# Six value pairs beside the second half's logits, and the last chunk's inverse step in three slots

## The chip, the cores and the metric

One core of one Trainium2 chip runs the whole program. The metric is device time in microseconds, the median of the runs shown. Engines are named as in the profile: PE (TensorE matmul), PEld (its weight load), DVE (VectorE), ACT (ScalarE), POOL (GpSimd) and SP (SyncE, which here only issues DMAs).

## The reference

Two independent computations share the program, and their outputs are put side by side.

```python
# A: sliding dilated attention, S = 2048, D = 640, 32 heads of 20, window 8, dilation 2
qkv = x @ wqkv                                   # split into q, k, v
logits[s, w] = q[s] . k[s - 2 w] * 20 ** -0.5    # w = 0..7, masked where s - 2 w < 0
attn = softmax(logits over w)
a = (sum over w of attn[s, w] * v[s - 2 w]) @ wo
# B: long convolution by FFT, L = 2048, D = 640, N = 192
K = Re(sum over n of Cc * exp(dt A l) * dt Bc)   # one filter of length 2048 a channel
y = irfft(rfft(pad(u)) * rfft(pad(K)))[:L] + u * Dskip
out = concatenate([a, y])
```

## The kernel before

Part B works in five chunks of 128 channels. For each chunk it makes the filter (DVE and PE), transforms it, multiplies it with the transformed input (`products`, L348, which loads the input's spectrum from `Sdram` and multiplies it on DVE into P1 and P2), and takes a first inverse step (`inverse_a`, L364). That step has four pieces. Each is 16 matmuls into a PSUM tile `ps_ia`, which ACT then copies to the tile Z (L375). After the fourth piece one DMA on SP's queue writes Z to `Zdram` (L377). The second inverse step (`Inverse.part`, L639, matmuls into `ps_ib`) needs, for one of four quarters of the output positions, the pieces of all five chunks, read back from `Zdram` and `UDdram` by 15 DMAs of 128 KB (`Inverse.load`, L629, issued at L637). Quarter 0's loads are spread over SP and POOL, those of quarters 1 and 2 all go to SP, and quarter 3 is spread again. There are 24 such parts, six to a quarter.

Part A stands beside and after the last chunk. The sequence is handled in two halves of 256 positions on each of four groups. `att.products` (L520, DVE) and `att.logits` (L523, 20 matmuls at L531) make the logits of one window offset w; every second w ACT moves them to SBUF (L534). `softmax_a` (L539) and `softmax_b` (L549) are DVE trees with one ACT exponential between them. Values are made per channel of a head, 20 in all: `proj_v` (L488) makes two channels at once in a two-bank PSUM tile (40 matmuls at L495, one ACT copy at L497), `proj_v1` (L499) one channel in a one-bank tile (20 matmuls, one copy at L506). `v_halo` (L508) copies the positions that a window reaches over a group's edge. `av_step` (L574) multiplies values with attention weights on DVE (L584) and sums over w on PE with identity matmuls (`ps_o`); `p2` runs in a ring of six buffers. `out_piece` (L596) is the output projection (`ps_op`).

The order around the change is partly a scheduler's and partly the program's. Before `att.in_order()` a scheduler places instructions on each engine by its own estimate, with the program's order as its guide. After that call every matmul of the attention object stays in program order (those matmuls all carry the line L420). DMAs are placed by the scheduler throughout, but each engine's queue issues its own in the order that it was given, and a DMA that waits holds up those behind it. SP's queue uses eight completion lanes in turn: a DMA waits until the one eight places before it has landed.

Before the change, the loop over w of the second half's logits (L770 to L783) does `transform(LAST)` at w = 0, `softmax_b(0)` at w = 2, `products` and all four pieces of `inverse_a` at w = 4, and a value pair at w = 1, 3, 5 and 7. Then come the halo of channels 0 to 7, the loads of quarters 0 to 2, and a second loop over w (L799), here called loop 2: `av_step` for the first half's channels 0 to 7, with two single channels each at w = 0 to 5 and four `ps_ib` parts and two halos at w = 4 and 5. After it five blocks of `av_step` follow (L815). The first of them, here called block 1, takes eight `ps_ib` parts, one a step; blocks 2 and 3 take pieces of the output projection instead.

Of the kernel before, what the change touches and what calls it, by code (L numbers as in the profile page):

```python
# [347 lines left out]
def products(tc, pools, Sk, Sd, pool, late):  # L348

    nc = tc.nc  # L350
    P1 = pool.tile([128, 32, 32, 4], bf16, name="P1", tag="sp", bufs=3)
    P2 = pool.tile([128, 32, 32, 4], bf16, name="P2", tag="sp", bufs=3)
    fl = lambda t: t.rearrange("p a b c -> p (a b c)")
    nc.sync.dma_start(out=fl(P1[:]), in_=Sd)
    nc.sync.dma_start(out=fl(P2[0:64]), in_=Sd[64:128])
    nc.sync.dma_start(out=fl(P2[64:128]), in_=Sd[0:64])
    for P in (P1, P2):
        ins = nc.vector.tensor_tensor(out=P[:], in0=P[:], in1=Sk[:], op=A.mult)  # L358
        if late:
            tc.keep_in_program_order(ins)  # L360
    return P1, P2, ins


def inverse_a(tc, pools, C, P1, P2, Zd, pool):  # L364

    nc = tc.nc
    MM = nc.tensor.matmul
    Z = pool.tile([128, 128, 32], bf16, name="Z", tag="sp", bufs=3)

    def piece(b):  # L370
        ps = pools["psum"].tile([128, 8, 128], f32, name="ps_ia", tag="bank2")
        for j in range(8):
            for w, P in enumerate((P1, P2)):
                MM(ps[:, j], lhsT=P[:, 8 * b + j].rearrange("p k g -> p (k g)"), rhs=C["EA"][:, w, :], start=(j % 4 == 0 and w == 0), stop=(w == 1), skip_group_check=True)  # L374
        nc.scalar.copy(out=Z[:, :, 8 * b:8 * b + 8], in_=ps[:].rearrange("p j x -> p x j"))  # L375
        if b == 3:
            nc.sync.dma_start(out=Zd, in_=Z[:].rearrange("p x j -> p (x j)"))  # L377

    return [lambda b=b: piece(b) for b in range(4)]
# [279 lines left out]
def body(tc, ctx, pools, prm, B_u, B_Dskip, Sd, Zd, UDd, A_x, A_wqkv, A_wo, out_a, out_b):  # L659
# [5 lines left out]
    fp = fft.enter_context(tc.tile_pool(name="fft", bufs=1, side="right"))  # L665
# [6 lines left out]
    C = dict(BD=BD, T2=T2, EA=EA, Dsb=Dsb, U=U)  # L672
    R, trig = {}, {}
    with tc.tile_pool(name="prep_b", bufs=1) as pb, tc.tile_pool(name="prep_c", bufs=1) as pc, tc.tile_pool(name="prep_a", bufs=1) as pa, tc.tile_pool(name="psum_p", bufs=2, space=bass.MemoryType.PSUM) as psp:
        pools.update(prep_a=pa, prep_b=pb, prep_c=pc)
        B, fill = partB_prep(tc, dict(pools, psum=psp), prm)
# [17 lines left out]
    att = Attention(tc, pools, A_x, A_wqkv, A_wo, out_a, psk, psg)  # L694
    Kb, Sk = {}, {}

    def transform(c):
        Sk[c] = fwd(tc, pools, C, (lambda ut: Kb[c][:, ut, :]), 1, fp)[0]
# [8 lines left out]
    LAST = NCH - 1  # L707
    for c in range(NCH):
# [6 lines left out]
        if c > 0:  # L715
            P1, P2, last = products(tc, pools, Sk[c - 1], Sd[c - 1], fp, True)
            ia = inverse_a(tc, pools, C, P1, P2, Zd[c - 1], fp)
# [52 lines left out]
    for w in range(W):  # L770
        if w >= 2:
            att.products(1, w)
        att.logits(1, w)
        if w == 0:
            transform(LAST)
        elif w == 2:
            att.softmax_b(0)
        elif w == 4:
            P1, P2, _ = products(tc, pools, Sk[LAST], Sd[LAST], fp, False)
            for f in inverse_a(tc, pools, C, P1, P2, Zd[LAST], fp):  # L780
                f()
        if w in (1, 3, 5, 7):
            att.proj_v(w - 1)  # L783
    att.v_halo(0, 8)
    fft.close()
    att.in_order()
# [4 lines left out]
    parts = inv.parts()  # L791
    rest = []

    def fill(some, n=1):
        for f in some[0:n]:
            f()
        del some[0:n]

    for w in range(W):  # L799
        if w < 6:  # L800
            att.proj_v1(8 + 2 * w)
            att.proj_v1(9 + 2 * w)
            if w in (4, 5):
                fill(parts)
                att.v_halo(*((8, 8) if w == 4 else (16, 4)))
                fill(parts)
        if w == 0:
            att.open_out(a2)
        att.av_step(0, 256, 0, 2, w)
        if w == 2:  # L810
            att.softmax_a(1)
        elif w == 4:
            att.softmax_b(1)
# [20 lines left out]
def kernel(  # L834
# [28 lines left out]
    Zd = dpool.tile([NCH, 128, 4096], bf16, name="Zdram")  # L863
    UDd = dpool.tile([NCH, 128, 2048], bf16, name="UDdram")
    body(tc, ctx, pools, prm, B_u, B_Dskip, Sd, Zd, UDd, A_x, A_wqkv, A_wo, out_a, out_b)


# [28 lines left out]
```

## Time and profile before

| | |
|---|---|
| median of 3 runs | 447.49 us (445.54 to 448.25) |
| the profiled execution's own time | 445.28 us |
| its span | 443.5 us |
| mean granted TensorE clock | 0.915 |
| busy: DVE, PE, ACT, POOL | 392.6, 358.7, 314.6, 41.1 us |
| DMA moved | 51.62 MB, mean 116 GB/s |

Busy time is summed over the whole span, and the stages differ much. The change touches what lies between about 336 and 392 us of the span. A row of the timeline gives start, length, engine, line, operation, output and input tile, count, and in brackets how long the engine was idle before and what ended that. A row SPq is the issue of a DMA on SP's queue, not its transfer.

### The profile page before, as it was taken

The numbers are of one execution on the slowest core, as the hardware profiler recorded it, in microseconds if no ns is written. First come the engines' busy times: TensorE is split into PE (matmuls) and PEld (weight loads), VectorE is DVE, ScalarE is ACT, GpSimd is POOL, SyncE is SP. The second block draws the span as 40 slices with busy tenths as digits, with TensorE's granted clock in tenths as the row PEclk, the third lists the DMA queues.
The fourth block names the chain that finished last, engine by engine and source line by source line (L and its number), as shares of the span: only waits on it lengthen the run. The fifth ranks groups of instructions, "written<-read, shape, count | busy, mean of one in ns | idle before, by whom it ended". The sixth has DMA issues, their size and how long they took to land.

```text
span 443.5 us, 17699 instructions
## 1 busy us (share of the span) xinstructions
PE 358.7 (81%) x8041; PEld 241.5 (54%) x8041; DVE 392.6 (89%) x394; ACT 314.6 (71%) x576; POOL 41.1 (9%) x85
## 2 busy tenths in 40 slices
PE   1385759989878987879687989899997679769896
PEld 0243656867755676457555665544556646424443
DVE  8889999999979999999999889669799989768751
ACT  3984999889998999799997815244486354635653
POOL 7440000000000000000010000000000030503110
PEclk9967888999896999699896989999999699959999
DMA  5589003171251404431299905200004097797243
GB/s 145 185 158 187 5 1 121 38 254 50 96 187 55 98 28 191 143 75 28 120 278 176 248 15 199 98 1 1 1 0 98 2 248 198 196 209 215 82 104 117
DMA packets 45131, 51.62 MB, mean 116 GB/s; under 512 B 31376, under 2 KB 38992, under 8 KB 42368
## 3 DMA queue, kind: packets, MB, share of 16 engines
q1 hardware_dynamic: 41520, 41.41, 35.5%
q0 software_dynamic: 3392, 8.95, 7.2%
q8 instruction: 63, 1.03, 1.0%
q10 hardware_dynamic: 144, 0.12, 0.1%
q14 instruction: 12, 0.10, 0.1%
HBM read 28.03 MB, written 18.35 MB: 105 GB/s over the span
## 4 chain that ended last, share of the span: by engine, by line
PE 44%; ACT 29%; DVE 11%; issue 6%; DMA 5%; SPq 4%; ACTq 0%; POOL 0%; DVEq 0%; POOLq 0%
ACT R L222 10%; ACT A L338 6%; PE ps_k L318 6%; PE ps_ph L247 6%; PE ps_k L323 6%; PE ps_op L420 6%; PE ps_k L464 5%; ACT Sg L344 4%; DVE prod L521 4%; PE ps_ph L250 4%; SPq L637 3%; PE ps_ia L374 3%; DMA Z<-Zdram 3%; PE ps_o L420 3%; PE ps_f L343 2%
## 5 line engine op out<-in xcount | busy, mean ns | idle before, releaser
L305 DVE TENSOR_TENSOR Y<-F,G 128x3072 bf16<-128x3072 bf16 x60 | 103.2, 1759 | 0.4 <-PE ps_k L323 0.3
L222 ACT ACTIVATE R<-LPC 128x192 bf16<-128x192 f32 x225 | 59.3, 359 | 0.1
L247 PE MATMUL ps_ph<-LPC 128*128 128x256 bf16 (+1 forms) x200 | 41.0, 308 | 20.5 <-DMA LPC<-lo 8.0
L318 PE MATMUL ps_k<-Y,X 128*32 128x64 bf16 x1920 | 47.0, 239 | 8.3 <-issue 4.5
L323 PE MATMUL ps_k<-Y,X 64*32 64x64 bf16 x1920 | 43.2, 234 | 2.9 <-issue 2.9
L318 PEld LDWEIGHTS <-X 128*32 128x32 bf16 x1920 | 32.1, 117 | 18.1 <-issue 9.7
L344 ACT CAST Sg<-ps_f 128x1024 bf16<-128x1024 f32 x40 | 37.6, 1025 | 5.8 <-PE ps_f L343 5.8
L338 ACT CAST A<-ps_f 128x1024 bf16<-128x1024 f32 x40 | 37.6, 1032 | 1.6 <-PE ps_f L337 1.4
L584 DVE TENSOR_TENSOR prod<-v,atp 128x2048 bf16<-128x2048 bf16 (+2 forms) x32 | 31.3, 1021 | 8.3 <-PE ps_o L420 5.6
L255 ACT ACTIVATE TX<-ps_ph 128x864 bf16<-128x864 int16 (+1 forms) x40 | 32.3, 864 | 8.2 <-DVE X L271 3.9
L271 DVE TENSOR_TENSOR X<-R,TX 128x1536 bf16<-128x1536 bf16 x40 | 36.5, 958 | 0.0
L343 PE MATMUL ps_f<-A,T 128*128 128x128 bf16 x320 | 23.9, 236 | 14.9 <-ACT A L338 13.5
L323 PEld LDWEIGHTS <-X 64*32 64x32 bf16 x1920 | 29.5, 113 | 11.4 <-issue 4.2
L255 ACT ACTIVATE TA<-ps_ph 128x768 bf16<-128x768 int16 x40 | 30.4, 822 | 2.7 <-PE ps_ph L250 2.4
L247 PEld LDWEIGHTS <-LPC 128*128 128x128 bf16 x200 | 15.1, 102 | 29.0 <-issue 14.1
L343 PEld LDWEIGHTS <-T 128*128 128x128 bf16 x320 | 21.9, 106 | 16.5 <-issue 15.5
L521 DVE TENSOR_TENSOR prod<-ql,kT 128x1024 bf16<-128x1024 bf16 (+1 forms) x24 | 23.1, 1039 | 8.3 <-ACT ql L483 8.3
L250 PE MATMUL ps_ph<-LPC 128*64 128x128 bf16 (+1 forms) x400 | 29.6, 248 | 0.0
L420 PE MATMUL ps_op<-wo,o 128*128 128x320 bf16 x160 | 28.1, 312 | 0.8 <-ACT o L594 0.4
L610 ACT CAST ob<-ps_op 128x320 bf16<-128x320 f32 x28 | 11.9, 431 | 22.1 <-PE ps_op L420 20.4
L375 ACT CAST Z<-ps_ia 128x1024 bf16<-128x1024 f32 x20 | 19.3, 1014 | 11.5 <-PE ps_ia L374 11.5
L374 PE MATMUL ps_ia<-EA,P 128*128 128x128 bf16 x320 | 24.1, 238 | 3.2 <-DVE P L358 3.2
(133 smaller groups left out, 658.8 us busy)
## 6 DMA issues: line engine op xcount, KB each, us to landing
Sdram<-Sg SPq DMA_DIRECT2D x5, 1024.0 KB
P<-Sdram SPq DMA_DIRECT2D x5, 1024.0 KB
P<-Sdram SPq DMA_DIRECT2D x10, 512.0 KB
Zdram<-Z SPq DMA_DIRECT2D x5, 1024.0 KB
Z<-Zdram SPq DMA_DIRECT2D x30, 128.0 KB
U<-in_B_u_dram SPq DMA_DIRECT2D x4, 640.0 KB
UDdram<-UD SPq DMA_DIRECT2D x10, 256.0 KB
out_dram<-ysb SPq DMA_DIRECT2D x32, 80.0 KB
```

The lines of the kernel that those rows point to most:

```text
L222: nc.scalar.activation(out=R[:, :, e, :], in_=src, func=ACT.Exp, scale=m)
L247: MM(o[:, :, 0:32], lhsT=L[:, 0:128], rhs=rhs, start=first, stop=last, skip_group_check=True)
L250: MM(o[64 * hh:64 * hh + 64, :, 32:48], lhsT=L[:, 128:192], rhs=rhs[:, :, 16 * hh:16 * hh + 16], start=False, stop=last, skip_group_check= ...
L255: last = nc.scalar.activation(out=dst[:, qs, e0:e0 + 2 * n, :].rearrange("p q (b e) f -> p b e q f", b=2), in_=words.rearrange("p b (e q f ...
L305: nc.vector.tensor_tensor(out=Y[:].rearrange("p q (b a) f -> p q b a f", a=8), in0=fa, in1=gb, op=A.mult)
L318: MM(ps[32 * g:32 * g + 32, t], lhsT=X[:, q, 2 - k, :, f], rhs=Ys[k][:, q, :, f], start=(t == 0 and k == 0), stop=False, tile_position=(0, ...
L323: MM(ps[32 * g:32 * g + 32, t], lhsT=X[hb, q, 2 - k, :, f], rhs=Ys[k][hb, q, :, f], start=False, stop=(k == 2), tile_position=(64 * (g // ...
L338: nc.scalar.copy(out=A1[:, :, 32 * b:32 * b + 32].rearrange("p k (j g) -> p k j g", g=4), in_=ps[:].rearrange("p j k g -> p k j g"))
L343: last = MM(ps[:, kk], lhsT=C["T2"][:, 8 * b + kk, :], rhs=A1[:, 8 * b + kk, :], start=(kk % 4 == 0), stop=True, skip_group_check=True)
L344: nc.scalar.copy(out=Sg[:, :, 8 * b:8 * b + 8, :], in_=ps[:].rearrange("p k (j g) -> p j k g", g=4))
L420: self.MM = lambda *a, **k: self.tc.keep_in_program_order(self.nc.tensor.matmul(*a, **k))
L521: self.nc.vector.tensor_tensor(out=self.prod[w % (4 - 2 * hf)][:, c0:c1], in0=self.q[hf][:, c0:c1], in1=self.kT[:, hf, c0:c1, :, HALO - DI ...
```

## The change

The order of the value pairs changes. Channels 0 to 11 are now made in pairs within the logits loop: pairs 0, 2, 4, 6, 8 and 10 at w = 1, 2, 3, 4, 5 and 7. The four pieces of the last chunk's `inverse_a`, which all stood at w = 4, are now spread: the first at w = 5 after its value pair, the second at w = 6, the last two at w = 7 after pair 10. The write of Z goes with the last piece. Loop 2 makes the eight channels that are left, at w = 0 to 3, with the halos at w = 3 and 4, and takes five `ps_ib` parts instead of four (one at w = 4, two at w = 5, one each at 6 and 7). No instruction is added or taken away except that two pairs are made by `proj_v` in place of four single channels by `proj_v1`; the matmul count is the same.

```diff
         elif w == 4:
             P1, P2, _ = products(tc, pools, Sk[LAST], Sd[LAST], fp, False)
-            for f in inverse_a(tc, pools, C, P1, P2, Zd[LAST], fp):
+            ia = inverse_a(tc, pools, C, P1, P2, Zd[LAST], fp)
+        if w > 0 and w != 6:
+            att.proj_v((0, 0, 2, 4, 6, 8, 0, 10)[w])
+        if w >= 5:
+            for f in ia[w - 5:w - 4] if w < 7 else ia[2:]:
                 f()
-        if w in (1, 3, 5, 7):
-            att.proj_v(w - 1)
     att.v_halo(0, 8)
...
     for w in range(W):
-        if w < 6:
-            att.proj_v1(8 + 2 * w)
-            att.proj_v1(9 + 2 * w)
-            if w in (4, 5):
+        if w < 4:
+            att.proj_v1(12 + 2 * w)
+            att.proj_v1(13 + 2 * w)
+        if w in (3, 4, 5):
+            if w > 3:
                 fill(parts)
-                att.v_halo(*((8, 8) if w == 4 else (16, 4)))
+            if w < 5:
+                att.v_halo(*((8, 8) if w == 3 else (16, 4)))
+            else:
                 fill(parts)
+        if w > 5:
+            fill(parts)
```

In the built program the change moves these on each engine. PE: the second pair now stands ahead of the logits of w = 3, pairs 4 and 6 ahead of and behind those of w = 4, pair 8 on both sides of those of w = 5; then the first `ps_ia` piece, logits 6, the second piece, logits 7, pair 10, the last two pieces, the halo. DVE: the first `av_step` product goes ahead of the second half's `softmax_a`. ACT: the copies follow PE's order; the first of them for block 2's output pieces now stands ahead of the copy of part 13. SP: five loads of quarter 1 now stand ahead of the write of Z, and quarter 0's loads behind it. POOL: unchanged but for one load of quarter 3, which goes ahead of the first output.

## The prediction

> **What bounds the kernel now.** I read the timelines of PE, SP and POOL from 335 us to the end first, then DVE and ACT, then the stage table (busy time, granted clock and DMA share) and the DMA view.
>
> The hole that the change fills is on PE:
>
> ```profile
> 339.35 2.33 PE L495 MATMUL ps_v<-xT,wv 128*32 128x512 bf16 x39
> 343.87 0.73 PE L531 MATMUL ps_l<-prod,Gs 128*32 128x256 bf16 x20 [2.19 <-DVE prod L521]
> 346.07 0.50 PE L374 MATMUL ps_ia<-EA,P 128*128 128x128 bf16 x3 [1.47 <-DVE P L358]
> 348.28 5.45 PE L374 MATMUL ps_ia<-EA,P 128*128 128x128 bf16 x61 [1.70 <-DVE P L358]
> ```
>
> PE waits 5.4 us in three places for DVE, which is busy without a break from 330 to 354. Later, from 361.5 to 380.7, it is the other way round: PE makes six pairs of single channels, and DVE waits 2.70 us (to 381.31) for the last of them.
>
> What runs beside that are the last chunk's loads:
>
> ```profile
> 354.82 0.33 SPq L377 DMA_DIRECT2D Zdram<-Z  x1
> 357.34 1.92 SPq L637 DMA_DIRECT2D Z<-Zdram  x3
> ...
> 361.86 3.64 SPq L637 DMA_DIRECT2D Z<-Zdram  x2
> ...
> 387.59 9.08 SPq L653 DMA_DIRECT2D out_dram<-ysb  x8
> ```
> ```profile
> 354.33 1.13 POOL L637 DMA_DIRECT2D Z<-Zdram  x2 [36.59 <-ACT Z L375]
> 360.37 0.56 POOL L637 DMA_DIRECT2D Z<-Zdram  x1 [2.71 <-DMA Zdram<-Z]
> 380.95 2.29 POOL L569 DMA_DIRECT2D wo<-in_A_wo_dram  x4 [20.02 <-PE ps_ib L420]
> ```
>
> The reader is to see that both queues start the moment Z is written, and that chunk 4's load on POOL waits for that write (landed by 360.37, 5.5 us after issue). SP then issues 38 loads until 387.3; its lanes tell the landings. The second load of the row at 361.86 went at 364.96, when the first quarter-1 load of 357.34 had come back; quarter 0's last load had landed by 371.98, quarter 1's by 381.40, quarter 2's by 396.20, each being the time of the issue eight places later.
>
> ```profile
> 382.60:391.80 9.20, 7.82 (x244) 3.08 (x219) 9.20 (x12) 6.20 (x12) 3.95 (x8) 0.71 1.04 229
> 391.80:395.30 3.50, 0.02 (x8) 0.02 (x7) 1.76 (x3) 1.04 (x3) 0.00 (x0) 0.50 1.11 239
> 395.30:400.00 4.70, 4.70 (x54) 1.82 (x54) 2.15 (x3) 0.85 (x2) 0.07 (x1) 0.50 0.71 153
> 400.00:434.60 34.60, 32.27 (x707) 15.70 (x705) 23.70 (x24) 20.65 (x43) 6.51 (x12) 1.00 0.50 136
> ```
>
> The columns are the stage, its length, busy PE, PEld, DVE, ACT and POOL, granted clock, DMA share and GB/s. From 395.3 to 434.6 PE is busy 37 of 39.3 us: what counts for the end is when PE starts block 2. Ahead of that stand 3.5 us in which PE does nothing (to 395.28, put down to "issue", between the 6th and 7th of 16 matmuls) while the DMA engines are full.
>
> **The change, step by step.**
>
> *PE's hole, gain.* Pair 4, pair 6 and two fifths of pair 8 (2.2, 2.2 and 0.9 us by the 2.33 us row) go into the hole. But logits 5 and the rest of pair 8 now stand ahead of the first `ps_ia` matmul, and logits 5 needs a DVE product that is ready only at 350.9. So `ps_ia` starts at about 353, not 348.28; the hole is moved to 347.5 to 351, not closed. Logits 7 ends near 357.2 instead of 358.0, and the first `av_step` product (1.2 us) fits into DVE's wait of 1.46 us for the logits' copy; DVE ends `softmax_b(1)` at 377.5 instead of 378.6.
>
> *Loop 2, gain.* Four pairs of singles instead of six, 2.68 us each with their `ps_o` (365.99 to 368.68): 5.4 us of PE less, and the start stays (the first copy still follows the exponential at 363.4). The last value is copied near 374.6 instead of 381.28, DVE's 2.70 us wait goes, and block 1 could start at 377.6 instead of 381.31. On these two steps alone the kernel gains 3.7 us.
>
> *The write of Z, loss.* The last two pieces come after pair 10: logits 7 to 357.2, pair 10 to 359.4, then 32 matmuls at 56 ns (the last 14 of the row above took 0.78 us) or about 100 ns at half clock, to 361.2 to 362.6. ACT copies at 1.01 us each, so the write goes at 362.2 to 363.8. I take 363.0, 8.2 us late. POOL's six quarter-0 loads, which wait for the same memory, go 8 us late too. On SP only five quarter-1 loads stand ahead of the write (356.6 to 359.6); behind it, blocked for 3.4 us, are all the other 33 loads, quarter 0's eight among them, and the output writes.
>
> *Quarter 0.* Ten loads, quarter 0's last the tenth, follow the write as ten did before. By the same spacing, landed by 371.98 becomes 380.2. But PE gives up the value weights at 373.5 instead of 380.65, so POOL issues `wo` (4 x 200 KB) and seven loads of quarter 3 from 373.8, into this traffic. What that costs SP's loads:
>
> ```profile
> q0 software_dynamic: 542, 1.60, 58.1%
> q1 hardware_dynamic: 1478, 1.15, 47.2%
> ```
>
> These are POOL's and SP's queues over 383 to 395 (packets, MB, share): SP's moved 1.15 MB in 12 us, 1.37 us a load, against 0.63 us (its issue spacing from 371.98 to 375.06). Some four of the ten would pay this, 3 us. Bounds for the landing of quarter 0: 378 (before's 371.98, less 2 us in which the lane may have been free already, plus 8.2) to 386 (all ten at 1.37 us from 372). I take 381.6. PE has its first `ps_ib` part next at 374.0, so it stands still for 7.6 us; there was no such wait before, as quarter 0 was there by 371.98 and the part ran at 376.25. DVE fills its ring of six and stops near 379.3.
>
> *Block 1.* After 381.6 PE needs 3 us at full or 5 at half clock for what is left of loop 2, so it enters block 1 at 385 to 387 against 382.64: the 3.7 us are gone. Part 7, at the block's second step, needs all of quarter 1.
>
> *Quarter 2, the step that decides.* Loop 2 takes five parts instead of four, so block 1's last part is now part 13, the first of quarter 2; before, that ran at 416.1. It stands ahead of block 2 in PE's order, so block 2 can't start before quarter 2 has landed. Two ways to that time. By shift: before, 41.4 us from the write's issue (354.82) to 396.20. After, five loads (0.64 MB, 3.1 us at the 208 GB/s of 362 to 372) are out of the way early; the traffic no longer thins out between 371.98 and 381 (180 GB/s with a gap of some 2.5 us, 4 us in all); one POOL load more, 0.6 us. 363.0 + 41.4 - 3.1 - 4 + 0.6 = 397.9. By rate: the first load behind the write lands at 373.1 (364.96 was 10.1 us after the write); five more by 376 at 0.63 us; nine or ten at 1.37 us beside POOL's 1.7 MB (13 us, to 389); the other 18 at 0.6 us: 400. I take 399, from 396 (no loss beside POOL) to 404 (quarter 0 at its upper bound, all else behind it). Quarter 1 is there by 391, and PE ends block 1 near 397, so quarter 2 is the later one.
>
> *The sum.* Block 2 starts at 399.0 instead of 395.28: +3.7 us. The 3.5 us of idle PE fall into the wait for quarter 2 and are not paid twice. One `ps_ib` part (0.33 us) less stands in the last block: -0.3. Block 2's first steps ran at half clock before (0.50 until 400) and, PE having waited, should again. In sum +3.4, rounded to 3.5: on the profiled execution's 445.28 us that is 448.8. That execution is 2.2 us faster than the median of the runs shown, so on the median I forecast 447.49 + 3.5 = 451.0 us.
>
> The Trainium skill (Runtime: NRT & Kernel Launch, Instruction fetch mechanics) says that an engine's instructions are refilled in blocks of 16 KiB, 256 instructions, and that this is hidden behind the rate of issue. The DMA view has 63 instruction packets of 1.03 MB in all, which fits; hidden it is not, if the 3.5 us are such a refill held up by full DMA engines, as I read them. If the page is right they have another cause, and rival C follows.
>
> **The rivals.**
>
> A. *The loads are hidden, and the gain arrives.* If quarter 0 is there at 374 and quarter 2 by 391, PE starts block 1 at 377.6 and ends it, at DVE's 0.87 us a product, 5 us before 391.3. 447.49 - 5 = 442.5, faster. For it: the transfers before had a thin stretch. Against: 33 loads, the write and 2.6 MB of POOL's in 28 us are 8 MB, 280 GB/s, where full stretches of these loads show 208 to 239.
>
> B. *The traffic is late, but less: no change.* If quarter 2 lands near 396, block 2 starts where it did: 447.5 - 0.3 + 0.7, 448. For it: the sum by bytes gives 397.9, and PE could come to block 2 at a full clock (up to -2 us).
>
> C. *The idle 3.5 us come again, behind the wait.* Then block 2 starts at 402.5, and the time is 454.5. For it: they have no releaser in the trace. Against: they came with full DMA engines, which by 400 have drained.
>
> D. *POOL's early `wo` starves SP throughout.* All of quarter 0's loads at 1.37 us put everything 5 us later: 404, 456. It decides from the point where `wo` is issued before the first load behind the write has landed (373.8 against 373.1, close).
>
> **How the numbers follow.** My forecast (quarter 2 decides, 397.5 to 401) has 0.45, A 0.10, B 0.20, C 0.12, D 0.13. A measurement of this kernel tells about 1% from no change: 443.0 and 452.0. Faster by over 1% is most of A, 0.08; slower by over 1% is C, D and two fifths of the forecast, which reaches from 449.3 to 453, 0.43; the rest 0.49. The range goes from 444.0 (a part of A) to 456.0.
>
> **What would show it.** Right: PE idle for several us ahead of the first `ps_ib` part (near 374 to 381) and again ahead of the 13th, each put down to a DMA or to "issue"; the write of Z issued near 363; POOL's `wo` near 374; DVE's wait of 2.70 us gone, with a longer one near 379 in its place; PE busy without a break from block 2 on. Wrong: the first `ps_ib` part at once after the halo near 374, or block 2 ahead of 395, or a write of Z before 361.

## The result, and the profile after

The changed kernel takes 451.62 us (median of 20 runs, 448.24 to 455.61), against 448.05 us for the kernel before (20 runs, 444.67 to 449.84). The ratio is 1.0083, 95% interval 1.0055 to 1.011: slower by 0.8%, some 3.7 us. Single executions of one kernel differ by up to some 2%, and now and then one falls into a slower state; the ratios leave those out, while the medians in us are of all runs. The profiled execution took 452.38 us, its span is 450.6 us, the granted clock 0.908.

This execution lags before's already at a place that the change does not touch. The first wait of PE in the second half's logits (a row of four `ps_l` matmuls after 0.53 us of idle) stands at 331.10 us here and stood at 328.93 before. I call the difference, 2.17 us, the offset, and take it off wherever a time of this trace is set against one of before ("on before's clock"); the other kernels get their own offset from the same row.

PE's timeline of the changed kernel, in the order that the prediction went through. Columns: start, length, engine, line, operation, output and input tile, shape, count, and in brackets the idle time before and what ended it.

```profile
353.18 0.76 PE L531 MATMUL ps_l<-prod,Gs 128*32 128x256 bf16 x20 [3.39 <-DVE prod L521]
...
356.43 1.40 PE L374 MATMUL ps_ia<-EA,P 128*128 128x128 bf16 x16
...
382.33 0.59 PE L420 MATMUL ps_ib<-Z,HB 96*32 96x160 bf16 x12 [5.87 <-DMA Z<-Zdram]
...
388.37 0.52 PE L420 MATMUL ps_o<-prod,ident 32*32 32x384 bf16 x8 [0.86 <-ACT o L594]
...
393.85 0.59 PE L420 MATMUL ps_ib<-Z,HB 96*32 96x160 bf16 x12 [4.09 <-DMA Z<-Zdram]
...
401.99 0.59 PE L420 MATMUL ps_ib<-Z,HB 96*32 96x160 bf16 x12 [2.35 <-DMA out_dram<-ysb]
402.50 0.55 PE L420 MATMUL ps_o<-prod,ident 32*32 32x384 bf16 x16
```

The rows of before at the same places are these:

```profile
376.25 0.38 PE L420 MATMUL ps_ib<-Z,HB 96*32 96x160 bf16 x12
...
382.64 0.36 PE L420 MATMUL ps_o<-prod,ident 32*32 32x384 bf16 x8
...
391.27 0.51 PE L420 MATMUL ps_o<-prod,ident 32*32 32x384 bf16 x6
395.28 0.53 PE L420 MATMUL ps_o<-prod,ident 32*32 32x384 bf16 x10 [3.49 <-issue]
```

They are the first part without a wait, the entry into block 1, the end of block 1, and block 2's first step, which the 3.49 us cut in two. In the changed kernel the three `ps_ib` rows with a wait are the first part (all of quarter 0 needed), part 7 (quarter 1) and part 13 (quarter 2); the last row is block 2's first step. Together PE stands still 12.31 us for the read-back of Z, where before it did so nowhere ahead of block 2. The releaser of the last wait is named as an output write, which a part does not read. The output writes use the same eight completion lanes as the loads (a lane is a counter that a waiting engine reads). Quarter 2's last load was issued at 398.74, its lane counted it as landed at 401.85, and PE's wait on that lane ended then; so it is quarter 2 that PE waited for. The queues of the same kernel (SPq and POOL rows are issues of DMAs):

```profile
365.29 0.34 SPq L377 DMA_DIRECT2D Zdram<-Z  x1
...
398.74 0.59 SPq L637 DMA_DIRECT2D Z<-UDdram  x1
399.42 5.59 SPq L653 DMA_DIRECT2D out_dram<-ysb  x8
```
```profile
364.80 1.13 POOL L637 DMA_DIRECT2D Z<-Zdram  x2 [44.89 <-PE ps_h L517]
...
372.88 0.56 POOL L637 DMA_DIRECT2D Z<-Zdram  x1 [4.75 <-DMA Zdram<-Z]
376.40 2.29 POOL L569 DMA_DIRECT2D wo<-in_A_wo_dram  x4 [2.96 <-PE ps_h L420]
```

The write of Z goes at 363.1 on before's clock (354.82 before), and POOL's load of the fifth chunk is free to go 7.6 us after it (5.5 before). POOL's `wo` follows at 374.2 on that clock (380.95 before). What the stages hold (stage, length, busy PE, PEld, DVE, ACT, POOL with counts, granted clock, DMA share, GB/s):

```profile
376.46:382.33 5.87, 0.00 (x0) 0.03 (x1) 4.18 (x3) 0.42 (x2) 4.44 (x8) 0.89 1.12 229
...
389.76:393.85 4.09, 0.00 (x1) 0.10 (x1) 1.06 (x2) 0.00 (x0) 0.00 (x0) 0.50 1.01 234
...
399.64:401.99 2.35, 0.01 (x2) 0.04 (x2) 1.08 (x2) 1.50 (x2) 0.00 (x0) 0.50 0.78 211
401.99:441.80 39.81, 37.57 (x766) 17.96 (x767) 25.92 (x26) 21.60 (x45) 6.01 (x11) 0.92 0.51 135
```

In the first two waits the DMA engines are full (share 1.12 and 1.01), and both waits end with a load of Z. From the start of block 2 PE is busy 37.57 of 39.81 us, as it was before. So the loss is made ahead of block 2 and carried to the end.

### The profile page after: what moved, and what is told of

Its sections match the earlier page's. It is cut to its first block, busy times and chain, and to the rows that moved or that the text cites. A ratio compares the mean times of both kernels' runs of the same rounds, so it can differ in the third digit from the quotient of the medians.

```text
span 450.6 us, 17696 instructions
## 1 busy us (share of the span) xinstructions
PE 363.5 (81%) x8041; PEld 243.2 (54%) x8041; DVE 393.1 (87%) x394; ACT 314.6 (70%) x574; POOL 40.5 (9%) x85
## 3 DMA queue, kind: packets, MB, share of 16 engines
q8 instruction: 63, 1.03, 1.0%
## 4 chain that ended last, share of the span: by engine, by line
PE 40%; ACT 27%; issue 12%; DVE 12%; DMA 5%; POOL 1%; SPq 1%; DVEq 0%; ACTq 0%; POOLq 0%
ACT R L222 10%; PE ps_k L318 6%; PE ps_ph L247 6%; ACT A L338 6%; PE ps_k L323 6%; PE ps_k L464 5%; DVE prod L521 4%; ACT Sg L344 4%; PE ps_ph L250 4%; PE ps_f L343 3%; PE ps_op L420 3%; ACT Z L375 2%; PE ps_ia L374 2%; DVE X L271 2%; DMA wo<-in_A_wo_dram 2%
## 5 line engine op out<-in xcount | busy, mean ns | idle before, releaser
L343 PE MATMUL ps_f<-A,T 128*128 128x128 bf16 x320 | 26.2, 252 | 14.1 <-ACT A L338 13.2
L343 PEld LDWEIGHTS <-T 128*128 128x128 bf16 x320 | 24.4, 115 | 15.4 <-issue 14.3
L250 PEld LDWEIGHTS <-LPC 128*64 128x64 bf16 x400 | 15.2, 117 | 19.1 <-issue 18.9
L324 ACT CAST Ksb<-ps_k 128x512 bf16<-128x512 f32 x20 | 11.5, 581 | 18.8 <-PE ps_k L323 18.8
```

What stands on the lines that cost most here:

```text
L250: MM(o[64 * hh:64 * hh + 64, :, 32:48], lhsT=L[:, 128:192], rhs=rhs[:, :, 16 * hh:16 * hh + 16], start=False, stop=last, skip_group_check= ...
L343: last = MM(ps[:, kk], lhsT=C["T2"][:, 8 * b + kk, :], rhs=A1[:, 8 * b + kk, :], start=(kk % 4 == 0), stop=True, skip_group_check=True)
```

## The experiments

All ratios are against runs of before beside the kernel's own on the same chip; where a quotient of two medians differs from the ratio, the ratio is used.

| kernel | us | ratio | interval |
|---|---|---|---|
| after | 451.62 | 1.0083 | 1.0055 to 1.011 |
| e1, pieces in one slot | 445.58 | 0.9978 | 0.9948 to 1.0009 |
| e2, only the spread | 449.08 | 1.0036 | 0.9999 to 1.0073 |
| e3, after with four parts in loop 2 | 449.51 | 1.0039 | 1.0001 to 1.0077 |
| e5, e1 and e3 together | 444.32 | 0.9896 | 0.9859 to 0.9933 |
| e4, after, Z written from ScalarE's queue | 449.41 | 1.0049 | 1.0018 to 1.0081 |
| e6, after, `wo` and quarter 3 on SP | 448.44 | 1.0002 | 0.9964 to 1.004 |
| e7, e5, `wo` and quarter 3 on SP | 442.56 | 0.9904 | 0.9864 to 0.9944 |
| e8, e7, `wo` ahead of quarter 2 | 440.81 | 0.9862 | 0.982 to 0.9904 |
| e9, e5, only quarter 3 on SP | 441.31 | 0.982 | 0.9768 to 0.9872 |
| e10, before with e8's queues | 445.33 | 0.9995 | 0.9949 to 1.004 |
| e11, e8 with after's spread | 445.41 | 0.998 | 0.9945 to 1.0016 |

**The change taken apart: e1, e2, e3, e5.** My theory was the prediction's: spreading the pieces makes the write of Z late, the fifth part in loop 2 puts quarter 2 ahead of block 2, and the moved value pairs in themselves are a gain. The rivals were that the value pairs cost something themselves, and that the idle time without a releaser comes again.

e1 keeps after's value pairs and puts all four pieces back at w = 4:

```diff
-        if w >= 5:
-            for f in ia[w - 5:w - 4] if w < 7 else ia[2:]:
+        if w == 4:
+            for f in ia:
                 f()
```


> The value pairs as in the changed kernel, the four inverse pieces all at w = 4 behind pair 6, so that they stand ahead of the logits of w = 5 on PE. Theory (the late write of Z delays the loads, and block 1 and block 2 wait for them): Z is written 2 to 3 us earlier than before the change, PE has no wait ahead of the first ps_ib part in loop 2, block 1 starts some 3 us earlier than before; part 13 is still the last of block 1 and waits for quarter 2, which lands 1 to 2 us earlier than before, so block 2 starts 0 to 3 us earlier and the time is 445 to 448, ratio 0.993 to 1.000. Rival (making six pairs beside the logits is itself what costs, by the hole on PE that is moved and the half clock behind it): 450 to 452, ratio 1.005 to 1.009. Rival (the loss is POOL's early wo in SP's loads, not the late write): the first ps_ib part waits still, 449 to 451.

e2 keeps before's value pairs and loop 2 and has only the spread (`ia[w - 5:w - 4]` at w = 5 and 6, `ia[2:]` at 7):

> The value pairs and loop 2 as before the change, only the four inverse pieces spread over w = 5, 6 and 7. Theory: Z is written about 6 us later than before (near 361), the loads follow, the first ps_ib part waits about 2 us where it did not wait, quarter 1 is late for part 7; part 13 is not in block 1, so quarter 2 decides nothing: 448.5 to 450, ratio 1.002 to 1.006. Rival (the pairs cost, the spread costs nothing): 447.5 to 448.2, ratio 0.998 to 1.001.

e3 is after with one part less in loop 2:

```diff
-        if w > 5:
+        if w == 6:
             fill(parts)
```


> The changed kernel with four ps_ib parts in loop 2 instead of five (none at w = 7), so that part 13, the first of quarter 2, is no longer in block 1. Theory: the wait of 2.4 us ahead of part 13 goes, the waits ahead of parts 1 and 7 stay; block 2 starts 2 to 3 us earlier than in the changed kernel: 448.5 to 450, ratio 1.001 to 1.005. Rival (that wait is a late block of instructions and comes again somewhere near): as the changed kernel, 451 to 452, ratio 1.007 to 1.010.

e5 has the edits of e1 and e3:

> Both edits together: six pairs beside the logits, the four inverse pieces at w = 4, four ps_ib parts in loop 2. Theory: no part waits for its loads, block 1 starts some 3 us earlier than before and block 2 with it, unless the idle 3.5 us ahead of block 2 grow: 442 to 446, ratio 0.987 to 0.996. Rival (the pairs cost): 450 to 452. Rival (block 2's start is set by the full DMA engines through PE's instructions, whenever PE comes there): 447 to 448, ratio 0.998 to 1.001.

The spread is what costs. Taking it back gives 1.05% with five parts (after to e1, 4.7 us) and 1.43% with four (e3 to e5, 6.4 us). e2, the spread alone on before, is slower by 0.4%, some 1.6 us, with an interval that reaches 1 (0.9999); its trace is not read here, so why the spread costs less on before's own order is not shown. The value pairs cost nothing: e5, which differs from before in nothing but their order and loop 2's, is 4.7 us faster (1.04%). Giving up the fifth part is worth 3.7 us without the spread (e1 to e5) and some 2.0 us with it (after to e3, where the intervals overlap). Why the spread costs, e1's PE rows show; its offset is -0.23 us:

```profile
373.48 0.39 PE L420 MATMUL ps_ib<-Z,HB 96*32 96x160 bf16 x12 [0.38 <-ACT v L506]
...
378.45 0.39 PE L420 MATMUL ps_o<-prod,ident 32*32 32x384 bf16 x16 [1.43 <-DVE prod L584]
...
393.15 0.74 PE L420 MATMUL ps_ib<-Z,HB 96*32 96x160 bf16 x12 [6.00 <-DMA out_dram<-ysb]
393.82 0.55 PE L420 MATMUL ps_o<-prod,ident 32*32 32x384 bf16 x16
```

With Z written in time (SP's issue of L377 stands at 352.92) quarter 0 is there when PE comes, PE enters block 1 at 378.7 on before's clock instead of 382.64, and then part 13 waits 6.00 us for quarter 2. Most of the gain ends there: block 2 starts at 394.05 on before's clock, 1.2 us ahead of before, where PE had entered block 1 4.0 us ahead. e3 has no part of quarter 2 ahead of block 2, and keeps the other two waits (6.14 us for quarter 0, put down to `wo`, which a part does not read, and 3.92 us for quarter 1):

```profile
378.30 0.59 PE L420 MATMUL ps_ib<-Z,HB 96*32 96x160 bf16 x12 [6.14 <-DMA wo<-in_A_wo_dram]
...
389.96 0.59 PE L420 MATMUL ps_ib<-Z,HB 96*32 96x160 bf16 x12 [3.92 <-DMA Z<-Zdram]
...
395.18 1.10 PE L420 MATMUL ps_o<-prod,ident 32*32 32x384 bf16 x16
```

Its offset is -1.11 us, so block 2 starts at 396.3 on before's clock, 1.0 us late, where after has 400.3. e5 has none of the three waits but for 0.34 us. What is left in it is idle time that nothing releases:

```profile
375.52 0.39 PE L420 MATMUL ps_ib<-Z,HB 96*32 96x160 bf16 x12 [0.34 <-DMA Z<-UDdram]
...
380.27 0.55 PE L420 MATMUL ps_o<-prod,ident 32*32 32x384 bf16 x16 [1.69 <-DVE prod L584]
...
385.62 0.51 PE L420 MATMUL ps_o<-prod,ident 32*32 32x384 bf16 x6 [1.96 <-issue]
...
390.28 0.51 PE L420 MATMUL ps_o<-prod,ident 32*32 32x384 bf16 x6
391.83 0.53 PE L420 MATMUL ps_o<-prod,ident 32*32 32x384 bf16 x10 [1.03 <-issue]
```

**The queues: e4, e6, e7.** Open was how much of the loss is the queue's order (33 DMAs behind the write on SP) and how much the traffic that POOL adds beside SP. e4 lets ScalarE, which makes Z, issue the write:

```diff
-            nc.sync.dma_start(out=Zd, in_=Z[:].rearrange("p x j -> p (x j)"))
+            (queue or nc.sync).dma_start(out=Zd, in_=Z[:].rearrange("p x j -> p (x j)"))
...
-            ia = inverse_a(tc, pools, C, P1, P2, Zd[LAST], fp)
+            ia = inverse_a(tc, pools, C, P1, P2, Zd[LAST], fp, nc.scalar)
```


> After, with the last chunk's write of Z issued by ScalarE, which makes the data, in place of SP. In after SP is free at 363.3 us, holds the write until 365.29 and has every load of quarter 0 but POOL's behind it. Theory (the lateness of the data is the cost, the wait of the queue only a small part of it): ScalarE issues the write within half a microsecond of its last copy, near 365.3, so the write gains nothing; SP's eight loads of quarter 0 go some 2 us sooner, the first part of quarter 0 waits 1 to 3 us less than 5.87, and the whole comes to 449 to 451.5 us, ratio to before 1.002 to 1.008. Rival (what stands behind the write in SP's queue is the whole loss): no loss is left, 447 to 448.5. Rival (the loads of the fifth chunk alone decide): 451 to 452, the first wait as in after.

The time is where the theory put it, but not by the way it named. The write left at 362.97, which on after's clock is 365.2, no sooner, as expected. But SP did not go on beside it:

```profile
363.68 2.80 SPq L637 DMA_DIRECT2D Z<-Zdram  x2
371.40 0.31 SPq L637 DMA_DIRECT2D Z<-UDdram  x1
```

SP issued twelve loads from 356.46 to 366.48, the last four of them quarter 0's, and then stood still for 4.9 us until the write had landed (371.39). The write now goes from ACT's queue, but it counts on one of the same eight lanes, and quarter 0's fifth load needed that lane. It went at 373.6 on after's clock, where in after itself it went at 371.6. The write took 8.42 us to land (7.04 in after), and quarter 0 was complete at 382.4 on after's clock, against 381.6. So the first part waited 8.09 us, not less than 5.87: PE came to it 1.4 us earlier, and it started at 383.2 on after's clock, later than in after (382.33). The wait for quarter 1 fell to 0.92 us, and part 13 still waited 2.20. The interval overlaps after's. As SP was not free in e4, it doesn't decide what the place of the write on SP is worth. After's own trace bounds it for quarter 0: POOL's load of the fifth chunk, which has to wait for the write on any queue, landed at 380.50, and quarter 0's last load, one of SP's, at 381.60, so if POOL's load keeps its time, SP's order costs quarter 0 at most 1.1 us.

e6 is after, with POOL's eleven loads behind quarter 0 (four of `wo`, seven of quarter 3) put on SP; e7 does the same to e5:

```diff
-            nc.gpsimd.dma_start(out=self.wo[32 * dd:32 * dd + 32], in_=wsrc[dd])
+            nc.sync.dma_start(out=self.wo[32 * dd:32 * dd + 32], in_=wsrc[dd])
...
-                (nc.sync, nc.gpsimd)[(c + ri) % 2 if qr in (0, 3) else 0].dma_start(...
+                (nc.sync, nc.gpsimd)[(c + ri) % 2 if qr == 0 else 0].dma_start(...
```


> After, with wo's four loads and all of quarter 3's put on SP, behind quarter 2's, so that POOL loads nothing beside SP once quarter 0 is there. Theory (in after POOL's eleven loads from 376.4 on take rate from SP's quarters 1 and 2): the wait ahead of quarter 0 stays near 6 us, those ahead of quarter 1 (4.09 us) and quarter 2 (2.35 us) go or fall below 1 us in sum, an idle stretch without a wait of 1 to 3.5 us can come back ahead of block 2, and the time is 446 to 449 us, ratio 0.995 to 1.003. Rival (all bytes share one rate and their order by queue doesn't matter, or SP's issue is the limit): quarter 2 is as late as in after, 451 to 453. Rival (wo comes too late behind quarter 2): block 2's first output piece waits 2 to 5 us for it, 451 to 455.

> e5_one_slot_four_parts with the same two edits of the queues as e6_one_queue_after_quarter_0. Theory: there no part of block 1 waited for a transfer, so less load beside it frees nothing there; what is left are the idle stretches without a wait, 1.96 and 1.03 us, that came while the transfers were full, so 443 to 444.5 us, ratio to before 0.987 to 0.992. Rival (those stretches come from the instructions alone, not from the traffic): 444 to 445 and the same two stretches at the same place. Rival (wo, or quarter 3, comes too late in one queue): 446 to 449 with a wait for wo or Z in block 2 or later.

In e6 the wait for quarter 0 stays and those for quarters 1 and 2 are gone but for 0.56 us, as the theory said. The rival that `wo` comes too late came true as well, for 2.99 us. The PE rows of e6:

```profile
379.76 0.59 PE L420 MATMUL ps_ib<-Z,HB 96*32 96x160 bf16 x12 [5.65 <-DMA Z<-Zdram]
...
393.46 0.68 PE L420 MATMUL ps_ib<-Z,HB 96*32 96x160 bf16 x12 [0.56 <-DMA Z<-UDdram]
397.61 1.49 PE L420 MATMUL ps_op<-wo,o 128*128 128x320 bf16 x5 [2.99 <-DMA wo<-in_A_wo_dram]
```

The ratio falls from 1.0083 to 1.0002: POOL's traffic is the larger part of what quarters 1 and 2 cost. The queues' own account agrees. From 376 to 402 us of after, SP's queue moved 3.75 MB beside POOL's 1.87 MB, 0.91 us for each load of 128 KB; in the same window of e11 below, where POOL moved 0.30 MB, SP's moved 4.98 MB, 0.68 us each. In e7 the one wait in block 2 is 4.65 us for `wo`; the time, 442.56 us, is below what any theory had for it, though its ratio lies where the first theory put it, and by its interval e7 is no better than e5.

**Giving `wo` the right place: e8, e9.** Quarter 2 can give way, as with four parts in loop 2 it is first read behind block 2. e8 puts its loads behind `wo`'s, e9 leaves `wo` on POOL and moves only quarter 3:

```diff
-    for qr in range(3):
+    for qr in range(2):
         inv.load(qr)
...
             att.open_out(a2)
+            inv.load(2)
```


> e7_best_one_queue with quarter 2's loads put behind wo's on SP (inv.load(2) after open_out). Quarter 2 is first read by the 13th part, which with four parts in loop 2 stands in the third block or later, so it can give way. Theory (e7's block 2 stood 4.65 us for wo, which came only behind fifteen loads of quarter 2): that wait goes, part of it comes back as idle stretches without a wait (1 to 3 us, as in e5), and the time is 439 to 442 us, ratio to before 0.981 to 0.988. Rival (the 4.65 us lay over idle that comes anyway): no change against e7, 442 to 443.5, with 3 to 5 us of PE idle without a wait near 390. Rival (quarter 2 is now late): a wait for Z of 2 us or more in block 2, 443 to 446.

> e5_one_slot_four_parts with quarter 3's loads on SP and wo's left on POOL: it parts the two edits of e7_best_one_queue. Theory (what stays of the traffic beside SP is wo's four loads; quarter 3's seven early ones on POOL are the larger part): wo is there early, no wait for it, idle stretches without a wait of 1 to 3 us stay, 441 to 444 us, ratio 0.984 to 0.991. Rival (only wo beside SP's loads matters): as e5, 444 to 445.5, with 1.96 and 1.03 us of idle at the same places. Rival (quarter 3's loads come too late from SP): a wait for Z after 410 us, 445 to 448.

Both are clearly faster than before, by 1.4% and 1.8%, and not told apart from each other. In e8 nothing of block 1 and block 2 waits for a transfer, and the idle without a releaser is gone from both blocks: at the matmul before which e5 stopped for 1.03 us, e8 goes on at once. (The row of 1.10 us holds a pause of 0.55 us, in which PE waits for ACT's copy of `ps_o`; the same row stands in e3, at 395.18 above.)

```profile
386.08 1.10 PE L420 MATMUL ps_o<-prod,ident 32*32 32x384 bf16 x16
387.12 1.51 PE L420 MATMUL ps_op<-wo,o 128*128 128x320 bf16 x5
```

e9 keeps one stretch without a releaser, of 0.93 us. With quarter 3 out of the way, then, it no longer matters measurably that `wo`'s four loads come from POOL. That quarter 3's seven loads alone account for the step from e5 is likely but not shown, as the intervals of e5 and e9 overlap (e5's reaches down to 0.9859, e9's up to 0.9872). Nor is e8 told apart from e5.

**Do the queues alone do it, and what does the spread cost then: e10, e11.** e10 is before with e8's queue edits, e11 is e8 with after's spread.

> Before with the queue edits of e8_wo_ahead_of_quarter_2 alone (wo's and quarter 3's loads on SP, wo ahead of quarter 2): no value pair and no piece is moved. Theory (what PE lost ahead of block 2 in before, 3.49 us without a wait, comes of the traffic that POOL's eleven loads add beside SP's): that stretch falls to 1 us or less and the time to 443 to 446 us, ratio 0.990 to 0.996. Rival (the stretch comes of the instructions alone): it stays at 3 us or more, 447 to 449. Rival (wo or quarter 3 too late): 448 to 452 with a wait for wo or Z.

> e8_wo_ahead_of_quarter_2 with after's spread of the four inverse pieces over three slots in place of one, and nothing else changed: what the spread alone costs when POOL no longer loads beside SP. Theory (the late write makes quarter 0 late, whatever POOL does): the first part waits 5 to 6.5 us for quarter 0, nothing further waits, and the time is e8's 440.8 plus 4 to 6, 445 to 447 us, ratio 0.994 to 1.000. Rival (the spread hurts only by way of the traffic behind it): 440.5 to 442.5.

e10 fell short of my theory: the 3.49 us ahead of block 2 are gone, and block 2 starts 5.0 us earlier than in before (392.45, offset 2.14), but the ratio is 0.9995. (The median, 445.33 us, does lie where the theory had it; it is 0.994 of the median of all runs of before beside it.) From block 2's start to the end it takes 53.25 us, where before took 48.22, so in the two traces what was won is lost again there. SP's rows of e10 tell one reason:

```profile
376.59 0.60 SPq L637 DMA_DIRECT2D Z<-UDdram  x1
382.49 2.52 SPq L569 DMA_DIRECT2D wo<-in_A_wo_dram  x4
```

SP stood still for 5.3 us because `wo`'s buffer holds what the value matmuls read until the last of them is made, which in e10 ends at 382.45, and everything behind it was late. Quarter 3's last load, issued by SP at 415.48, landed at 420.02, and a part waits 2.45 us for it:

```profile
420.21 0.84 PE L420 MATMUL ps_ib<-Z,HB 96*32 96x160 bf16 x12 [2.45 <-DMA out_dram<-ysb]
```

The other part of the loss is PE itself: from block 2's start to the end it is busy 46.15 us at a granted clock of 0.85, in before 42.25 us at 0.95. Why the clock was lower is not shown; e5, e9 and e11 have 0.86 to 0.87 there, e8 and e3 have before's 0.95. In e8 SP issues `wo` at 373.95, at once behind the load before it: only with the value pairs moved forward does the new order of the queue fit. Whether the 2.45 us come from that stop alone was not tried.

e11 came out as expected: 5.25 us of wait for quarter 0, then none for a transfer above 0.2 us, and 1.18% more than e8, some 5.3 us (each of the two ratios is known to 0.4%). With the value pairs moved forward, three pairs of kernels now give the spread alone 4.7, 6.4 and 5.3 us; on before's own order, e2 gives 1.6 us, not clear of zero.

## Why the prediction was right, step by step

*PE's hole.* Right: moved, not closed. PE waits 3.39 us for logits 5, which start at 351.0 on before's clock (said 350.9). The first piece starts at 354.3 instead of 353.

*Loop 2's gain.* Right, and shown by itself: without a late write PE enters block 1 at 378.7 on before's clock (e1 and e5), in before at 382.64, and DVE's first product of the block stands at 377.7, where I had 377.6. In before it was this:

```profile
381.31 3.56 DVE L584 TENSOR_TENSOR prod<-v,atp 128x1536 bf16<-128x1536 bf16 x4 [2.70 <-ACT v L506]
```

DVE's wait of 2.70 us is replaced by one of 2.99 us that ends at 383.67 in after. The cause of the new wait was not the one I gave. DVE did not fill its ring of six; it stopped after a single product of block 1, because the next needs the halo copy that stands behind the waiting part:

```profile
379.73 0.95 DVE L584 TENSOR_TENSOR prod<-v,atp 128x1536 bf16<-128x1536 bf16 x1
383.67 1.83 DVE L584 TENSOR_TENSOR prod<-v,atp 128x1536 bf16<-128x1536 bf16 x2 [2.99 <-ACT v L518]
```

It cost nothing further, as PE was the later of the two.

*The write of Z.* Right: 363.1 against 363.0, with five loads ahead of it and POOL 8.3 us late. SP stood behind it for 2.0 us (to 365.29), where I had 3.4.

*Quarter 0.* The first part starts at 380.2 (said 381.6), after 5.87 us of idle (said 7.6). The surcharge for POOL's traffic, 3 us, was too much. From the issue of the write to the landing of quarter 0's last load it took 15.9 us in before (354.82 to 370.72), 16.3 in after, 15.9 in e6 and 15.7 in e11, the last two without POOL's later loads: that traffic costs quarter 0 some 0.4 us. I had the landing before at 371.98, the next issue on its lane; it was 1.3 us earlier. From there, 8.2 us for the late write and 0.4 us for the traffic give 379.3; quarter 0 was complete at 379.4 on before's clock, and the part starts 0.7 us behind it. The load that ended the wait was SP's, issued at 375.08 and landed at 381.60; POOL's load of the fifth chunk (issued at 372.88) landed at 380.50.

*Block 1.* Entered between 384.8 and 386.2 (said 385 to 387), left at 397.5 (said 397). I had quarter 1 there "by 391"; it was 391.7, and the 4.09 us that PE waits for it belong to the cost: e3, which has no wait for quarter 2, still starts block 2 1.0 us late.

*Quarter 2 decides.* Right: part 13 is the last wait ahead of block 2, at 399.8 (said 399). e3 gives its share, some 2.0 of 3.7 us, with intervals that overlap; e1 shows the same part alone, without a late write, using up most of the gain of the value pairs.

*The sum.* Block 2 starts at 400.3, 5.0 us late, where I had 3.7. The term that was mis-sized is the last: I set block 2's start equal to quarter 2's landing, but part 13 itself stands between (401.99 to 402.50, 0.5 us), and the landing was 0.7 us later than I took. The profiled execution ends 4.9 us later on before's clock; over the runs the ratio gives 3.7 us (2.5 to 4.9), against 3.5 forecast. That this comes so near is in part luck: the two traces lie further apart. The rest of the difference between the two profiled executions, the offset, lies ahead of all that was changed.

*The idle 3.5 us.* Right that they fall into the waits: no stretch without a releaser is left between the first part and block 2 of after, so rival C fell.

*The other rivals.* A fell with the three waits, though its mechanism (no loads in the way) is what e8 and e9 bring about, at 440.81 and 441.31 us. B is excluded by the interval. D took SP's loads at 1.37 us throughout; from 376 to 402 they took 0.91 us, and quarter 0 paid 0.4 us. Its direction was right, as e6 shows: taking POOL's loads away is worth 0.8%.

## What to carry to other kernels

A step that feeds a long chain of transfers should not be moved back to fill a hole ahead of it: here 5.4 us of idle PE were rearranged, and 4.7 to 6.4 us were paid for the 8 us by which one DMA write went later (on before's own order of the value pairs e2 shows 1.6 us, not clear of zero). When work is moved forward, look at what it releases: the early value pairs freed `wo`'s buffer, and POOL's queue at once sent data that was needed later into the traffic that was needed first. Read which consumer of a queue's data comes next before choosing the order of the loads; e5, which keeps the write early and quarter 2 behind block 2, has 1.0%, and e8 and e9, with the queues' order changed too, have 1.4 and 1.8%; what the queues add to e5 is not clear of the noise.

## What the runs showed of the hardware

PE's idle stretches that nothing releases stand a fixed number of instructions apart. In before (0.34 us, to 386.60, and 3.49 us, to 395.28) and in e5 (1.96 us, to 385.62, and 1.03 us, to 391.83) there are exactly 128 matmuls and 128 weight loads between the two, 256 instructions. The traces of before, after and all experiments but e2 have 119 such stretches of over 0.15 us; counted in PE's instructions, those of one trace all lie a multiple of 256 apart, to within one. Each ends 1.2 to 1.7 us after a packet of 16 KB of the instruction queue was through: in before those packets ended at 384.90 and 393.68, in e5 at 384.31 and 390.34. The Trainium skill (Runtime: NRT & Kernel Launch, Instruction fetch mechanics) says that instructions are refilled in blocks of 16 KiB, 256 instructions, and that this is mostly hidden behind the rate of issue. The distance and the packets agree with the refill; that it is hidden does not hold here. What makes a stretch long is not shown: the DMA engines' share was 1.05 to 1.11 in three of the four stretches named, but 0.55 in e5's of 1.03 us.
